# How a layer-norm and MLP kernel loads its first three raw tiles: half rows of 1,024 bytes in place of quarter pieces

## The chip, the cores and the metric

One Trainium2 chip, and on it one core: the kernel is a single program on core 0. The metric is device time in microseconds (us), from launch to end. TensorE does the matmuls, ScalarE the activation function and copies out of PSUM, VectorE (DVE) statistics, corrections and sums, GpSimd (POOL) small preparations; SyncE (SP) and ScalarE (ACT) issue the DMA transfers, each on its own queue.

## The reference

```python
B, S, D, F = 1, 2048, 1024, 3584          # all bf16
def reference(x, w1, b1, w2, b2):
    y = _layernorm(x, axis=-1)            # (x - mean) / sqrt(var + 1e-5)
    h = _gelu(jnp.einsum("bsd,df->bsf", y, w1) + b1)
    return jnp.einsum("bsf,fd->bsd", h, w2) + b2
```

## The kernel before

The 2,048 rows of `x` are 16 tiles of 128 rows, and four tiles are a block of 512 rows (`TB`). For each block the first layer makes 28 rows of `hT` (128 of the 3,584 columns of `w1` each), with eight accumulating matmuls per row, one for each 128-wide slice `dt` of D; then the second layer makes the output, and VectorE adds `b2`. Each engine's instructions stand in an order written out by hand; semaphores alone join them.

The change touches only the start, where the weights and `x` are still on their way. So that TensorE need not wait for layer-norm statistics, the first three tiles (`N_RAW`) enter the first layer as they are, transposed but not normalised. A column of ones beside them (column `RC`, 384) gives the column sums of `w1`, and VectorE corrects the results later, in PSUM, with each row's mean and deviation. Tile 3 takes the ordinary way: VectorE takes its statistics, normalises it (line 294), and only then is it transposed.

The parts of that start:

- **Loads.** `SP_FIRST_LOADS` and `ACT_FIRST_LOADS` (lines 28 and 29) are the order of issue on the two queues. `w0` to `w7` are slices dt 0 to 7 of the first seven rows of `w1`, 224 KB each. `x0p`, `x1p`, `x2p` are columns 0 to 255 of tiles 0, 1, 2 (64 KB each, 512 bytes a row); `xq` is columns 256 to 511 of all three tiles (192 KB), `xr` columns 512 to 1023 of all three (384 KB), `x3` is tile 3.
- **`warm(WARM)`, `warm(FILL)`.** 24 and 3 matmuls on constants, whose results nobody reads.
- **`pe_T`** (line 370). Transposes blocks of 128x128 on TensorE (line 378) into a PSUM bank; ScalarE copies them into `yT_sb` (line 391). A call names slices of D and tiles: `(0, 2, 1, 2)` is dt 0 and 1 of tile 1. Banks are "t", or "2_0" and "2_1", which two rows of the first wave take over afterwards.
- **`cells`** (line 518). Matmuls (line 416) of the first wave of `R` = 7 rows, for given rows, slices and tiles: 128 columns wide for one tile, 385 for all three and the ones. `first` is rows 0 to 4, `last2` rows 5 and 6, `every` all of them.
- **`act_cs`** (line 534). ScalarE copies the column sums of the wave's rows into `cs_sb` (line 536).
- **`late_row`** (line 557). Adds tile 3's part of a row, eight matmuls of 128 columns; it waits for the copies of tile 3's transposes and for `cs`. Behind late_row(0) and late_row(2) `pe_row` spreads the rows' means and deviations over the partitions (line 601), ScalarE copies them (line 604), and VectorE corrects row by row (lines 545 and 548).
- **Statistics.** VectorE takes those of the first halves (columns 0 to 511) of tiles 0, 1, 2, then of the second halves, then aggregates, then tile 3 (lines 266 and 274).

The stretch of the order that the change rewrites:

```python
        cells(first, (6,), 0, 3)
        pe_T([(0, 4, 3, 4), (4, 8, 3, 4)], "t")
        cells(first, (7,), 0, 3)
        act_cs(ps_1, 0, NB1, False)
        cells(last2, (6, 7), 0, 3)
        act_cs(ps_2, NB1, R, True)
        late_row(0)
```

## Time and profile before

| | |
|---|---|
| median of 3 runs | 397.53 us (397.34 to 397.7) |
| the profiled execution's own time | 397.77 us |
| its span, first to last instruction | 396.5 us |
| TensorE busy | 393.8 us, 1,999 matmuls |
| VectorE, ScalarE busy | 161.9 us, 84.2 us |
| DMA | 23.62 MB, nearly all of the loads in the first 57 us |

Times in the profile count from the first instruction of the span. A row of the timeline has start, duration, engine, line, operation, output and inputs, shape, count and, in brackets, the idle time of the engine ahead of it with what ended it. PE are the matmuls, PEld the weight loads that go with them; matmuls are pipelined, so that a matmul's listed duration reaches over the start of the next, and the spacing of starts is the pace. DMA issues are listed by engine with size and the time from issue to landing.

### The profile page before, as it was taken

How to read it: one execution, taken by the hardware profiler on the slowest of the kernel's cores; microseconds unless marked ns; L12 is line 12 of the kernel's file. 1: busy time of each engine (PE TensorE's matmuls, PEld its weight loads, DVE VectorE, ACT ScalarE, POOL GpSimd, SP SyncE). 2: the span in 40 equal slices, each digit the busy share in tenths (PEclk: the TensorE clock that was granted, in tenths of full speed). 3: DMA queues.
4: the chain of work that ended last, by engine and by line, in shares of the span. 5: the costliest groups of instructions: out<-in, count | busy, mean ns of one | idle time of the engine just before them, and what ended most of it. 6: DMA issues, size and time to landing. Idle time of an engine off the chain costs nothing.

```text
span 396.5 us, 4668 instructions
## 1 busy us (share of the span) xinstructions
PE 393.8 (99%) x1999; PEld 188.6 (48%) x1999; DVE 161.9 (41%) x343; ACT 84.2 (21%) x133; POOL 9.9 (2%) x28
## 2 busy tenths in 40 slices
PE   9999999999999999999999999999999999999998
PEld 7774444444444444444444444444444444444445
DVE  2798889988999705988100000001100000001011
ACT  3446430000143442000024433100003334400000
POOL 1100100002000200000000000000000000000000
DMA  7999950000000000000000000000000000000000
GB/s 243 361 378 387 385 185 15 26 26 16 26 0 2 0 0 2 26 15 26 26 15 0 0 2 0 13 15 26 14 27 13 2 0 0 2 13 26 15 26 26
DMA packets 17003, 23.62 MB, mean 60 GB/s; under 512 B 1240, under 2 KB 10584, under 8 KB 16984
## 3 DMA queue, kind: packets, MB, share of 16 engines
q1 hardware_dynamic: 16696, 23.05, 16.6%
q8 instruction: 15, 0.25, 0.3%
q10 hardware_dynamic: 288, 0.30, 0.2%
q14 instruction: 4, 0.03, 0.0%
HBM read 19.14 MB, written 4.19 MB: 59 GB/s over the span
## 4 chain that ended last, share of the span: by engine, by line
PE 99%; DVE 0%; issue 0%
PE ps L470 49%; PE ps L416 41%; PE ps_t L416 8%; PE ps L494 1%; PE ps_t L378 1%; PE ps L378 0%; PE ps_t L601 0%; DVE o_sb L481 0%
## 5 line engine op out<-in xcount | busy, mean ns | idle before, releaser
L470 PE MATMUL ps<-w_sb,hT_sb 128*128 128x512 bf16 (+2 forms) x924 | 194.1, 373 | 0.0
L416 PE MATMUL ps<-yT_sb,w_sb 128*128 128x512 bf16 (+3 forms) x862 | 167.9, 353 | 0.0
L470 PEld LDWEIGHTS ps<-w_sb,hT_sb 128*128 128x128 bf16 x924 | 89.3, 98 | 104.5
L416 PEld LDWEIGHTS ps<-yT_sb,w_sb 128*128 128x128 bf16 x862 | 80.0, 99 | 82.9
L425 ACT ACTIVATE hT_sb<-ps,b_sb 128x512 bf16<-128x512 f32 x94 | 64.3, 688 | 230.1 <-PE ps L416 217.2
L481 DVE TENSOR_TENSOR o_sb<-ps,b_sb 128x512 bf16<-128x512 f32 (+2 forms) x33 | 22.2, 674 | 198.4 <-PE ps L470 198.4
L354 DVE STREAM_TRANSPOSE yT_sb<-x_sb 32x256 bf16<-32x256 bf16 x192 | 83.7, 436 | 18.0 <-PE ps_t L416 15.0
L416 PE MATMUL ps_t<-yT_sb,w_sb 128*128 128x512 bf16 (+2 forms) x152 | 34.2, 368 | 0.0
L266 DVE BATCH_NORM_STATS2 st_sb<-x_sb 128x6 f32<-128x512 bf16 x32 | 20.8, 670 | 6.2 <-DMA x_sb<-in_x_dram 6.2
L416 PEld LDWEIGHTS ps_t<-yT_sb,w_sb 128*128 128x128 bf16 x152 | 14.6, 98 | 16.5
L425 ACT ACTIVATE hT_sb<-ps_t,b_sb 128x512 bf16<-128x512 f32 x18 | 12.4, 687 | 17.4 <-PE ps_t L416 14.6
L271 POOL TENSOR_TENSOR rstd_sb<-mv_sb,nhalf 128x1 f32<-128x1 f32 x13 | 7.1, 544 | 118.0 <-DVE mv_sb L274 117.5
L553 DVE TENSOR_TENSOR ps<-ps,row_sb 128x384 f32<-128x384 f32 x13 | 7.2, 561 | 3.1 <-PE ps L416 2.8
L294 DVE TENSOR_SCALAR x_sb<-x_sb,mv_sb,rstd_sb 128x1024 bf16<-128x1024 bf16 x13 | 7.1, 543 | 2.5 <-POOL rstd_sb L271 2.0
L545 DVE SCALAR_TENSOR_TENSOR ps<-row_sb,cs_sb,ps 128x385 f32<-128x385 f32 x11 | 6.8, 614 | 1.6 <-ACT row_sb L604 1.6
L548 DVE TENSOR_TENSOR ps<-ps,row_sb 128x385 f32<-128x385 f32 x11 | 6.2, 567 | 0.7 <-ACT row_sb L604 0.4
L391 ACT COPY yT_sb<-ps_t 128x384 bf16<-128x384 bf16 (+2 forms) x9 | 4.0, 493 | 8.2 <-PE ps_t L378 8.2
L494 PE MATMUL ps<-const-bfloat16-1.0 128*128 128x128 bf16 x27 | 3.2, 310 | 0.8 <-PEq L730 0.8
L334 DVE TENSOR_TENSOR yT_sb<-yT_sb,row_sb 128x1024 bf16<-128x1024 bf16 x3 | 3.6, 1215 | 0.0
L274 DVE BATCH_NORM_AGGREGATE mv_sb<-st_sb 128x2 f32<-128x15 f32 x16 | 3.2, 212 | 0.9
L494 PEld LDWEIGHTS ps<-const-bfloat16-1.0 128*128 128x128 bf16 x27 | 2.8, 144 | 0.8 <-issue 0.8
L378 PE MATMUL ps_t<-ident,x_sb 128*128 128x128 bf16 x28 | 2.5, 224 | 0.1
(40 smaller groups left out, 17.0 us busy)
## 6 DMA issues: line engine op xcount, KB each, us to landing
w_sb<-in_w_dram SPq DMA_DIRECT2D x4, 1792.0 KB, 18.1
out_dram<-o_sb SPq DMA_DIRECT2D x31, 128.0 KB, 1.7
x_sb<-in_x_dram SPq DMA_DIRECT2D x3, 1024.0 KB, 14.0
w_sb<-in_w_dram SPq DMA_DIRECT2D x2, 1024.0 KB, 9.5
w_sb<-in_w_dram SPq DMA_DIRECT2D x1, 2048.0 KB, 15.5
w_sb<-in_w_dram SPq DMA_DIRECT2D x7, 224.0 KB, 5.6
w_sb<-in_w_dram SPq DMA_DIRECT2D x1, 1280.0 KB, 16.3
x_sb<-in_x_dram SPq DMA_DIRECT2D x1, 384.0 KB, 5.5
```

Of the source, the lines that this page charges most:

```text
L266: return (lambda e, i=i, h=h: e.bn_stats(st_sb[:, i, 6 * h:6 * (h + 1)], x_sb[:, i, h * HC:(h + 1) * HC]), [x_ev[i][h]] + ([f"x{i}p"] if i ...
L271: pool.op(lambda e, i=i: e.tensor_tensor(out=rstd_sb[:, i:i + 1], in0=mv_sb[:, i, 1:2], in1=nhalf[:, i:i + 1], op=ALU.pow), waits=[f"mv{i} ...
L294: return (lambda e, i=i, c0=c0, c1=c1: e.tensor_scalar(out=x_sb[:, i, c0:c1], in0=x_sb[:, i, c0:c1], scalar1=mv_sb[:, i, 0:1], scalar2=rst ...
L354: res.append((lambda e, src=src, dst=dst: e.transpose(out=dst, in_=src), waits, (f"tr{i}" if lastop else None), 0.47))
L378: pe.op(lambda e, i=i, j=j, o=n * P: e.transpose(out=bap[:, o:o + P], in_=x_sb[:, i, j * P:(j + 1) * P], identity=ident[:, :]), waits=wait ...
L416: pe.op(lambda e: e.matmul(unit_bank(bank)[:, n0:n1], lhsT=w1_sb[:, dt, r * P:(r + 1) * P], rhs=yT_sb[:, buf, dt, n0:n1], start=start, sto ...
L425: act.op(lambda e, r=r, n0=n0, n1=n1, bank=bank: e.activation(out=hT_sb[:, r, n0:n1], in_=unit_bank(bank)[:, n0:n1], func=ACT.Gelu_apprx_tanh,
L470: pe.op(lambda e, st=st, ft=ft, c0=c0, c1=c1, bank=bank: e.matmul(ps_2[:, bank, 0:c1 - c0], lhsT=hT_sb[:, ft, st * P:(st + 1) * P], rhs=w2 ...
L481: crit.append((est[sig], (lambda e, ob=ob, c0=c0, c1=c1, bank=bank: e.tensor_tensor(out=o_sb[:, ob, c0:c1], in0=ps_2[:, bank, 0:c1 - c0], ...
L494: pe.op(lambda e: e.matmul(ps_1[:, 0, 0:P], lhsT=unit, rhs=unit, start=True, stop=True), waits=[gate] if gate else [])
L545: return [(lambda e: e.scalar_tensor_tensor(out=ap, in0=row_sb[:, 0, :], scalar=cs_ap[r], in1=ap, op0=ALU.mult, op1=ALU.add), [f"m1_0_{r}" ...
L553: crit.append((est[wait_ev], (lambda e: e.tensor_tensor(out=ap, in0=ap, in1=row_sb[:, 1, 0:RC], op=ALU.mult), [wait_ev, "row1"], f"sc_{r}" ...
```

## The change

Tiles 0, 1 and 2 are loaded by whole first halves, `x0a`, `x1a`, `x2a`: columns 0 to 511, 1,024 bytes a row, 128 KB each. `xq` is gone, and the order of the other loads stays. `x0a` is the first on SP, as `w0` is on ACT; `x2a` follows `w0` on ACT. All first-half statistics and the transposes of dt 0 to 3 now wait for a tile's own piece.

In TensorE's order tile 2's first transposes go into bank "t" rather than "2_1", and stand behind four of tile 0's seven cells; rows 5 and 6 follow in plain order. Tile 3's transposes move behind the first two cells of the last slice (dt 7), so that three cells of it and four of rows 5 and 6 are left between them and late_row(0), where there were five and four.

```diff
-SP_FIRST_LOADS = ("x0p", "x1p", "w1", "xq", "w2", "w3", "xr", "w4", "x3", "w5", "w6", "w7", "b1", "w8")
-ACT_FIRST_LOADS = ("w0", "x2p")
+SP_FIRST_LOADS = ("x0a", "x1a", "w1", "w2", "w3", "xr", "w4", "x3", "w5", "w6", "w7", "b1", "w8")
+ACT_FIRST_LOADS = ("w0", "x2a")
...
-            elif item[-1] == "p":
+            elif item[-1] == "a":
                 i = int(item[1:-1])
-                dma(x_sb[:, i, 0:QC], xf[i * P:(i + 1) * P, 0:QC], item, P * QC * 2)
-                x_ev[i] = ("xq", "xr")
+                dma(x_sb[:, i, 0:HC], xf[i * P:(i + 1) * P, 0:HC], item, P * HC * 2)
+                x_ev[i] = (item, "xr")
...
-                    [x_ev[i][h]] + ([f"x{i}p"] if i < N_RAW and h == 0 else []), f"st{i}_{h}", 0.65)
+                    [x_ev[i][h]], f"st{i}_{h}", 0.65)
...
-                    waits=waits + [raw_ev(i, j) if i < N_RAW else y_ev[i][j]],
+                    waits=waits + [x_ev[i][j * P // HC] if i < N_RAW else y_ev[i][j]],
...
         pe_T([(0, 2, 0, 1)], "t")
         warm(FILL)
         pe_T([(0, 2, 1, 2)], "2_0")
-        pe_T([(0, 2, 2, 3)], "2_1")
-        cells([*first, *reversed(last2)], (0,), 0, 1)
+        cells(every[:4], (0,), 0, 1)
+        pe_T([(0, 2, 2, 3)], "t")
+        cells(every[4:], (0,), 0, 1)
         cells(every, (0,), 1, 2)
         cells(every, (0,), 2, 3)
...
         cells(first, (6,), 0, 3)
+        cells(first[:2], (7,), 0, 3)
         pe_T([(0, 4, 3, 4), (4, 8, 3, 4)], "t")
-        cells(first, (7,), 0, 3)
+        cells(first[2:], (7,), 0, 3)
         act_cs(ps_1, 0, NB1, False)
         cells(last2, (6, 7), 0, 3)
```

More of the change, by code (lines that the diff above doesn't have):

```diff
@@ L111, in bass_standalone__mixer_channel_mlp__prompt_kernel @@
     assert DT == 8 and 0 < N_RAW < TPB
-    QC = 2 * P
     NR = max(R, min(RAW_ROWS, FT - 2))
@@ L212, in issue @@
         def issue(item):
-            if item in ("xq", "xr"):
-                c0, c1 = (QC, HC) if item == "xq" else (HC, D)
-                dma(x_sb[:, 0:N_RAW, c0:c1], xf[0:N_RAW * P, c0:c1].rearrange("(t p) d -> p t d", p=P), item,
-                    N_RAW * P * (c1 - c0) * 2)
-            elif item[-1] == "p":
+            if item == "xr":
+                dma(x_sb[:, 0:N_RAW, HC:D], xf[0:N_RAW * P, HC:D].rearrange("(t p) d -> p t d", p=P), item,
+                    N_RAW * P * HC * 2)
+            elif item[-1] == "a":
                 i = int(item[1:-1])
-                dma(x_sb[:, i, 0:QC], xf[i * P:(i + 1) * P, 0:QC], item, P * QC * 2)
-                x_ev[i] = ("xq", "xr")
+                dma(x_sb[:, i, 0:HC], xf[i * P:(i + 1) * P, 0:HC], item, P * HC * 2)
+                x_ev[i] = (item, "xr")
             elif item == "b1":
@@ L365, in bass_standalone__mixer_channel_mlp__prompt_kernel @@
         t_bank = {"t": ps_t[:, 0, :], "2_0": ps_2b[:, 0, :], "2_1": ps_2b[:, 1, :]}
-        def raw_ev(i, j):
-            return f"x{i}p" if j * P < QC else "xq" if j * P < HC else "xr"
         def pe_T(groups, bname):
```

## The prediction

> **What bounds the kernel now.** I read the page first: parts 1 and 4, busy time and the chain that ended last.

> ```profile
> PE 393.8 (99%) x1999; PEld 188.6 (48%) x1999; DVE 161.9 (41%) x343; ACT 84.2 (21%) x133; POOL 9.9 (2%) x28
> PE 99%; DVE 0%; issue 0%
> ```

> TensorE's own stream is the end of the kernel: the change can only save pauses between matmuls, or time that they run slowly. From the trace's list of matmul starts I subtracted the undisturbed spacing (0.163 us behind a 385-column one, 0.056 behind a 128-column one, 0.216 behind 512). From 5.9 us to the end all pauses add up to 0.40 us, and two make up 0.35 of it. The timeline of TensorE's weight loads shows both:

> ```profile
> 6.84 0.34 PEld L378 LDWEIGHTS ps_t<-ident,x_sb 128*128 128x128 bf16 x6 [0.38 <-DMA x_sb<-in_x_dram]
> 14.23 0.46 PEld L378 LDWEIGHTS ps_t<-ident,x_sb 128*128 128x128 bf16 x8 [0.39 <-issue]
> ```

> The first is the transposes of columns 256 to 511, which wait for `xq`. The matmul before started at 6.525, so the engine was free at 6.69 and began at 6.84: 0.15 us. The second is tile 3's transposes, which wait for its normalisation: free at 13.900 + 0.163 = 14.06, begun at 14.26: 0.20 us. The brackets count weight-load idle, part of which is normal.

> Next the stages of the start: us, then busy time and count of TensorE, weight loads, VectorE, ScalarE, GpSimd; granted clock; DMA share; GB/s.

> ```profile
> 2.40:3.00 0.60, 0.60 (x8) 0.60 (x7) 0.00 (x0) 0.58 (x1) 0.25 (x3) 1.00 0.98 341
> 3.60:4.00 0.40, 0.40 (x5) 0.39 (x5) 0.00 (x0) 0.03 (x1) 0.00 (x0) 1.00 0.93 314
> 4.00:4.60 0.60, 0.60 (x9) 0.59 (x7) 0.00 (x0) 0.44 (x2) 0.00 (x0) 1.00 0.40 99
> 4.60:5.20 0.60, 0.60 (x7) 0.45 (x5) 0.00 (x0) 0.55 (x2) 0.00 (x0) 1.00 0.69 109
> 5.20:5.80 0.60, 0.60 (x8) 0.60 (x7) 0.00 (x0) 0.00 (x0) 0.00 (x0) 1.00 0.79 218
> 5.80:6.40 0.60, 0.60 (x13) 0.60 (x11) 0.00 (x0) 0.00 (x0) 0.00 (x0) 1.00 1.09 352
> ```

> Two things are to be seen. TensorE gets through more 128-column matmuls per stretch behind 5.8 us than before it: their spacing falls there from 0.107 to 0.056 us, though the granted clock's column says 1.00 throughout. So a pause ahead of 5.8 costs only (0.107 - 0.056) less than it looks: each 0.107 us lost displaces one matmul, which is then done at 0.056, a factor of 0.52. And the DMA engines, at 314 to 341 GB/s before 4.0, fall to about 100 from 4.0 to 5.2, while `w1` and `xq` are on their way.

> Last, the work behind tile 3's transposes on ScalarE, and the VectorE steps ahead of them (start, duration):

> ```profile
> 14.90 1.07 ACT L391 COPY yT_sb<-ps_t 128x512 bf16<-128x512 bf16 x2 [2.07 <-PE ps_t L378]
> 15.86 0.18 ACT L536 COPY cs_sb<-ps 128x5 f32<-128x5 f32 x1
> ```

> ```profile
> 9.15 1.88 DVE L266 BATCH_NORM_STATS2 st_sb<-x_sb 128x6 f32<-128x512 bf16 x3 [0.45 <-DMA x_sb<-in_x_dram]
> ...
> 13.57 0.54 DVE L294 TENSOR_SCALAR x_sb<-x_sb,mv_sb,rstd_sb 128x1024 bf16<-128x1024 bf16 x1
> ```

> The small copy (`cs`, at line 536) ends at 16.05, and the first `late_row` starts at 16.17. That start is no wait yet: the matmul before began at 16.010, and 16.010 + 0.163 is 16.17. But the margin is only 0.12 us less the signal's own time, which an exposed wait for a ScalarE copy shows as 0.06 (copy done 5.15, matmul at 5.20). So late_row(0) can't be much over 0.06 us earlier while tile 3's transposes stay where they are.

> **The loads.** Removed are `xq` and the three 64 KB pieces; added are three of 128 KB. Bytes ahead of `w2`, `w3` and `xr` are the same (1,056 KB up to `w2`), so I leave these where they landed (7.39, 8.00, 9.12); one SP issue less (0.43 us of SP's time) brings nothing, since these issues end over 5 us ahead of the landings. `x0p` was issued at 0.79 and landed 2.64 later, at 3.43; `x1p` at 3.97, `x2p` at 4.15, `w0` at 3.72. For `x0a`, twice the bytes beside `w0`: between 3.43 (nothing lost) and 3.75 (lands with `w0`); I take 3.55, nearer the first, because the half-size piece landed 0.29 ahead of `w0`. All of `x0a`, `x1a`, `x2a` and `w0` is 608 KB against 416 before, 197 kB more; at 330 GB/s that is 0.6 us, so `x2a` lands by 4.75. For `x1a`: between 3.97 and 5.3 (caught in the thin stretch); I take 4.35, a third of the difference off `x2a`. `w1` landed at 6.25, 640 KB into the loads; now it is 832 KB in, without `xq` beside it: 5.4 to 6.5, and I take 6.2, before its matmuls need it.

> **TensorE up to 6.5 us.** The 24 warm-up matmuls end at 3.38. Before, the first transpose came at 3.56, 0.13 after the landing; now at 3.68: 0.12 us lost. Two transposes and three fillers take 5 x 0.107 = 0.53 to 4.21; tile 1's transposes wait for `x1a` until about 4.45: 0.24 lost. Four cells of tile 0 (0.43) now cover tile 2's load and its transposes; the bank of row 5 is no longer used for a transpose, so the wait for its copy (0.09 at 5.11 to 5.20) goes. Net 0.27 at the slow spacing, times 0.52: +0.14 us. Ends: no loss, -0.05 (only the bank wait goes), and +0.56 if `x1a` lands at 5.3 or later.

> **Behind 6.5 us.** Columns 256 to 511 are there already: -0.15. Tile 3's transposes stand two cells later (2 x 0.163 = 0.33): TensorE reaches them at 14.06 - 0.15 + 0.33 + 0.14 = 14.38, past 14.26, so the wait for `y` goes: -0.20. VectorE keeps its order; its first statistics start early, but its second ones still wait for `xr`, so `y` stays. But the move takes cover from the copies. From the start of tile 3's transposes to late_row(0) TensorE has 8 x 0.056 + 7 x 0.163 = 1.59 us of work (before, nine cells, 1.92), and the ScalarE chain takes 16.05 - 14.26 + 0.06 = 1.85. A new wait of 0.26 us stands ahead of late_row(0), on the `cs` copy; queued behind it are all late rows, row broadcasts and with them VectorE's corrections. Ends: 0.0, if the copies chain faster, and 0.33. Later waits have over 0.5 us of margin or move along with TensorE.

> Sum: +0.14 - 0.15 - 0.20 + 0.26 = +0.05 us. The profiled execution spans 396.5 and took 397.77, 1.27 outside the span; 0.24 over the median of 397.53. So the median should be 397.58; I say 397.6, no change. From 0.2% (0.8 us) on, a measurement of this kernel can tell a difference.

> **The rivals.** *The clock rises later (slower).* The fast spacing came at 5.8, 5.0 us after the first matmul and 2.3 after the pause that ended at 3.56. The change puts about 0.30 + 0.24 us of pauses into that stretch, where 0.18 + 0.09 were. If pauses of that size break it off, the rise comes 2.3 to 5.0 us after the one that ends at 4.45, at 6.7 to 9.4. Each us of slow spacing costs 1 - 0.52 = 0.48, so +0.4 to +1.7; I take 1.7, since the one rise that the trace shows from rest took 5.0: 399.2. It decides from a rise at 7.5 on (0.8 us). For it: nothing shows how much pause is borne. Against it: 0.27 was.
> [...]

> *The thin stretch catches the x pieces.* If the DMA engines thin out at 4.0 whatever is queued, `x1a` lands at 5.3, and `w1` after 6.5. TensorE then stands some 0.95 us more, less than half of it made up: +0.6, 398.1. For it: the fall came when the first 416 KB were through, and now 608 are wanted. Against it: then only `w1` and 512-byte rows were under way.

> *Faster.* All pauses go with nothing in their place: -0.35 - 0.14 = -0.49, 397.1. To pass 0.2% the clock must rise 0.65 us earlier as well (0.31/0.48): 396.7. Against it: the `cs` chain, and the pauses that late `x` pieces add.

> **How the numbers follow.** No change 0.59, its own range 397.1 to 398.0. Clock late 0.24, all slower. Thin stretch 0.12, a quarter of it over 0.2%. Faster 0.05. So slower 0.24 + 0.03 = 0.27, same 0.59 + 0.09 = 0.68, faster 0.05. The range must reach into the late clock to hold 8 in 10: 397.0 to 399.2.

> **What would show it.** Right: no pause ahead of the transposes of columns 256 to 511 and of tile 3; about 0.26 us ahead of late_row(0), ended by the `cs` copy; first transposes at about 3.7, tile 1's at 4.4; fast spacing from 5.8. Wrong: the spacing of 128-column matmuls still 0.107 behind 6 us; `xr` much earlier or later than 9.1; waits on `w1`.

## The result: slower by a third of a per cent, and the profile after

| | before | after |
|---|---|---|
| median of 22 runs each | 397.74 us (397.19 to 398.47) | 399.31 us (397.76 to 400.17) |
| profiled execution, its span | 397.77, 396.5 | 399.35, 398.1 |

The ratio is 1.0033, 95% interval 1.0022 to 1.0044: +1.6 us on the medians. The forecast was no change, 397.6. What came is the rival with the late clock, put at 399.2. The median of 22 lies 0.1 us past the upper end of the range, 399.2; the ratio times the 397.53 of the start is 398.8, inside it. The range reaches that far only to take in the rival: the forecast's own, 397.1 to 398.0, is missed. The single times after fall into two groups: seven at 397.76 to 397.90, one at 398.5, and fourteen at 399.09 to 400.17. Before, all lie within 1.3 us.

Page of the kernel after, parts 1 and 4:

```profile
PE 394.6 (99%) x1999; PEld 189.3 (48%) x1999; DVE 162.0 (41%) x343; ACT 84.3 (21%) x133; POOL 9.8 (2%) x28
PE 98%; DMA 1%; DVE 0%; issue 0%; ACT 0%
```

TensorE is still the end of the kernel, but a DMA now stands in its chain with 1%. The timeline shows where: the transposes of tile 0 and of tile 1, each behind a load.

```profile
4.21 0.37 PE L373 MATMUL ps_t<-ident,x_sb 128*128 128x128 bf16 x2 [0.67 <-DMA x_sb<-in_x_dram]
...
4.87 0.39 PE L373 MATMUL ps<-ident,x_sb 128*128 128x128 bf16 x2
```

The last warm-up matmul starts at 3.23 as before, and its place of 0.107 ends at 3.34. So TensorE stood 0.87 us ahead of the first transposes (before 0.22). The prediction has 3.38 for that end, and so 0.18 for the pause before; the difference of 0.65 is the same. Ahead of the second transposes it stood 0.17 us: the third filler started at 4.59, its place ended at 4.70. The stages of the start:

```profile
3.60:4.20 0.60, 0.00 (x0) 0.02 (x1) 0.10 (x1) 0.00 (x0) 0.00 (x0) 1.00 1.08 387
...
5.20:5.80 0.60, 0.60 (x9) 0.60 (x8) 0.60 (x2) 0.37 (x1) 0.00 (x0) 1.00 0.98 350
5.80:6.40 0.60, 0.60 (x8) 0.60 (x7) 0.33 (x1) 0.37 (x1) 0.00 (x0) 1.00 1.00 319
7.00:7.60 0.60, 0.60 (x8) 0.60 (x7) 0.00 (x0) 0.00 (x0) 0.00 (x0) 1.00 1.09 399
```

From 5.8 to 6.4 eight matmuls are under way where there were 13. The spacing is 0.107 us until 8.37 and 0.056 from there; before, that fell at 5.85. The granted clock's column says 1.00 throughout again. From 3.6 to 4.2 no matmul runs at all. The DMA engines keep 319 to 399 GB/s in these rows; the thin stretch of before (109 GB/s from 4.6 to 5.2) has shrunk to 224 to 260 there.

Behind that, the waits that were to go are gone, and the new one is there. Weight loads of TensorE, then ScalarE:

```profile
17.65 0.39 PEld L411 LDWEIGHTS ps<-yT_sb,w_sb 128*128 128x128 bf16 x7 [0.48 <-ACT cs_sb L531]
```

```profile
16.46 1.07 ACT L386 COPY yT_sb<-ps_t 128x512 bf16<-128x512 bf16 x2 [2.20 <-PE ps_t L373]
17.41 0.40 ACT L531 COPY cs_sb<-ps 128x5 f32<-128x5 f32 x2
```

The first copy of column sums ends at 17.60, and late_row(0) starts at 17.65; the matmul before it ended its place at 17.40, so the wait is 0.25 us.

### The profile page after: what moved, and what is told of

It reads as the page before. It is cut to its first block, busy times and chain, and to the rows that moved or that the text cites. A ratio compares the mean times of both kernels' runs of the same rounds, so it can differ in the third digit from the quotient of the medians.

```text
span 398.1 us, 4666 instructions
## 1 busy us (share of the span) xinstructions
PE 394.6 (99%) x1999; PEld 189.3 (48%) x1999; DVE 162.0 (41%) x343; ACT 84.3 (21%) x133; POOL 9.8 (2%) x28
## 4 chain that ended last, share of the span: by engine, by line
PE 98%; DMA 1%; DVE 0%; issue 0%; ACT 0%
PE ps L465 49%; PE ps L411 41%; PE ps_t L411 8%; DMA x_sb<-in_x_dram 1%; PE ps_t L373 1%; PE ps L373 0%; PE ps_t L596 0%; PE ps L489 0%; DVE o_sb L476 0%; ACT cs_sb L531 0%
```

## Experiments

Times are medians against the kernel before, run on the same chip (397.76 to 397.90). "Rise" is where the spacing of matmuls halves in the profiled execution, or where TensorE starts again if it stood then.

**The pause filled.** `-WARM = 24` `+WARM = 32` in the kernel after.

> The kernel after with 32 warm-up matmuls on constants ahead of the first transposes, where it has 24: 8 x 0.107 = 0.85 us more, so that they end at 4.23, when the first x piece is there (4.07 and the signal), and TensorE's first real work starts as late as in the kernel after. Theory (the pauses ahead of the x pieces delay the rise of TensorE's clock): the pause of 0.8 us is filled, the fast spacing comes at 5.8 to 6.5 instead of 8.4 and mostly in every execution, and the time falls by 0.9 to 1.2 us to about 398.1 to 398.4 or lower. Rival (the later loads themselves, with the waits that follow from them, cost the time): nothing of that moves, 399.3.

398.28 us (397.78 to 399.08), ratio 1.0010 (1.0002 to 1.0019); rise at 5.2. The first transposes start at 4.37, later even than in the kernel after, and the loads are the same (`x0a` at 4.24). About 1.0 of the 1.6 us is gone with eight matmuls that compute nothing, and so is the late group: apart from the profiled execution at 399.08 (span 396.8), no time is over 398.55. So the late loads as such don't carry the loss. What stays, 0.5 us, I put down to useful work that starts later. That isn't shown: with 28 warm-ups, below, it starts as late, at 4.40, and only 0.1 us stays.

**A pause alone.** `-WARM = 24` `+WARM = 16` in the kernel before, whose loads stay.

> The kernel before with 16 warm-up matmuls instead of 24: they end at 2.53, and TensorE stands 1.03 us until the first x piece, as the loads stay as they are. Theory (pauses delay the clock): the fast spacing comes up to 2.6 us later in most executions, the times spread into two groups, and the median rises by 0.8 to 1.7 us, to 398.5 to 399.4. Rival (the later loads cost the time, not the pause): no load moves and no useful matmul moves, 397.7 within 0.2.

398.46 us (397.91 to 398.98), ratio 1.0018 (1.0009 to 1.0026); rise at 8.1. Timeline of TensorE:

```profile
0.82 1.86 PE L494 MATMUL ps<-const-bfloat16-1.0 128*128 128x128 bf16 x16 [0.82 <-PEq L730]
3.51 0.37 PE L378 MATMUL ps_t<-ident,x_sb 128*128 128x128 bf16 x2 [0.83 <-DMA x_sb<-in_x_dram]
```

The first transposes come at 3.51, as in the kernel before, every useful matmul has its data when it had it or before, and the kernel is still slower by 0.7 us. The pause, 1.04 us here, delays the clock. The sum closes here too: the clock rises 2.2 us later, at 0.48 each 1.06 us, and with TensorE that late the waits for columns 256 to 511 and for tile 3 (0.15 + 0.20) are gone, though the loads are the old ones: 0.71, and the span grew from 396.54 to 397.22, by 0.68. The median came out just under the expected 398.5, and the two groups aren't to be seen.

**Tile 3's transposes alone.** In the kernel before:

```diff
         cells(first, (6,), 0, 3)
+        cells(first[:2], (7,), 0, 3)
         pe_T([(0, 4, 3, 4), (4, 8, 3, 4)], "t")
-        cells(first, (7,), 0, 3)
+        cells(first[2:], (7,), 0, 3)
```

> The kernel before with only tile 3's transposes moved two cells later. Theory (the clock carries the loss): the wait for tile 3's normalisation (0.20 us) goes and one for the small copy of column sums comes in its place; late_row(0) at 14.39 + 1.85 = 16.24 instead of 16.17, so +0.07 us, 397.7 to 397.9. Rival (the move of the transposes is what costs): a good part of the 1.6 us, at 398.5 or more.

397.93 us, ratio 1.0004 (0.9995 to 1.0013): within what was expected, and not to be told from before. The wait for the normalisation is gone and the one on `cs` has come, 0.25 us, ended by `cs` at line 536.

**The same edit undone in the kernel after.**

> The kernel after with tile 3's transposes back behind the cells of slice 6. Theory (the clock carries the loss): the wait of 0.25 us ahead of late_row(0) goes, the normalised tile 3 is there long before, so -0.2 us, and the late clock stays: about 399.1, still in two groups. Rival (the move of the transposes is what costs): back near 397.8.

398.79 us (397.55 to 400.01), ratio 1.0023 (1.0008 to 1.0038), six times at 397.55 to 398.12 and six at 399.47 to 400.01. The early group starts 0.2 us lower than in the kernel after, as expected, and the trace has no wait on `cs`; of the late group that can't be said. The groups stay, and the median between them says little. In the profiled execution the clock rises at 10.0, and TensorE doesn't wait for the normalisation of tile 3 either.

**A smaller pause.** `-WARM = 24` `+WARM = 20` in the kernel before, and `-WARM = 24` `+WARM = 28` in the kernel after.

> The kernel before with 20 warm-up matmuls: TensorE stands 0.6 us ahead of the first x piece, between the 0.2 of the kernel before and the 1.04 of the one with 16. Window theory (the clock is released at the end of a stretch of about 3.4 us in which TensorE stood no more than some limit, and those stretches run freely of the kernel; the traces put the limit between 0.40 us, which was borne, and 1.04, which was not): if 0.6 + 0.1 is borne, the times are those of before, 397.8 within 0.2; if not, the median is at 398.3 or more as with 16. Rival (any pause delays the rise by about its own length or more): half of the loss of 16 warm-ups, 398.1.

No trace up to then shows the stretch of about 3.4 us that the first expectation takes; that of the split load, below, has 3.41.

398.02 us (397.49 to 398.82), ratio 1.0007 (0.9998 to 1.0015): between the two expectations, and not to be told from the kernel before. The rise is at 7.2 in the trace (398.30 us).

> The kernel after with 28 warm-up matmuls: 0.43 us of the first pause is filled, 0.45 to 0.5 stays, and 0.17 ahead of tile 1. Window theory (up to about 0.8 us in one window is borne): no late group, at most 398.8, median about 398.2, like 32 warm-ups. Rival (the delay grows with the pause): halfway between 398.28 with 32 and 399.31 with 24, 398.8, with times over 399.

397.98 us (397.68 to 398.45), ratio 1.0004 (0.9995 to 1.0012), rise at 5.8. The late group is gone with half the pause filled, and the time is that of 32 warm-ups or less. A loss in proportion to the pause (398.8) is out.

**The kernel after, twice more.**

> The kernel after once more, for one more trace of it. Window theory: the loads land as they did (x0a at 4.1, x1a at 4.8) and the pauses are the same, but the fast spacing comes at another time: either by 4.9 (time about 397.8) or at 8.3 to 10.2 (399.1 to 400.2). Rival (a set number of undisturbed matmuls): 8.4 again, 399.3.

> The kernel after a third time, for the same question: the fast spacing by 4.9 with about 397.8, or at 8.3 to 10.2 with 399.1 to 400.2 (windows that run freely of the kernel); 8.4 and 399.3 again (a set number of matmuls).

399.17 with the rise at 8.0, and 399.48 with 8.6. `x0a` landed at 4.12 and 4.20, and the pauses are near those of the first trace (together 1.08 and 1.16 us, there 1.04); the rises differ by 0.6 us, and the times with them. So no set number of matmuls releases the clock, which would have given 8.4 again. The first is earlier than the 8.3 that I had given. No early execution was caught.

**Tile 0 in two pieces.** In the kernel after, `x0p` being columns 0 to 255 of tile 0 and `x0q` columns 256 to 511 (shown is the start of the order of loads; the first transposes wait for `x0p` alone):

```diff
-SP_FIRST_LOADS = ("x0a", "x1a", "w1", ...
+SP_FIRST_LOADS = ("x0p", "x0q", "x1a", "w1", ...
```

> The kernel after with tile 0's first half in two pieces of 512-byte rows, one behind the other on SP (64 KB each), the first of which alone the first transposes wait for. Theory (the first load is late because it is twice as long beside w0): the first piece lands at 3.4 to 3.5 as before, the first transposes start at 3.6, and the pause moves to tile 1's, which land at 4.8 or later: from 4.1 on, 0.7 us or more. By the window theory 0.2 + 0.7 is about as much as 1.04, so the loss stays largely, 398.5 to 399.3, in two groups. Rival (the pause ahead of the first transposes alone matters): 397.7 to 397.9. Where the second piece lands tells what the row length costs: at 4.07 the bytes count alone, later the shorter rows cost.

400.28 us (398.05 to 401.68, six runs), ratio 1.0060 (1.0038 to 1.0083): worse than any expectation. The first piece landed at 3.48 and the second at 4.0, but `x1a`, behind them, at 5.8: the thin stretch is back (74 to 110 GB/s from 4.2 to 4.8). TensorE stood 2.0 us ahead of tile 1's transposes. This trace holds a record of the granted clock, and so do five others, from the clock's first change on. Ahead of that, and in the traces without a record, the column reads 1.00 even where the spacing is slow, 0.107 us. The pause, and the column by stages:

```profile
5.87 0.28 PE L377 MATMUL ps<-ident,x_sb 128*128 128x128 bf16 x2 [1.79 <-DMA x_sb<-in_x_dram]
```

```profile
6.66:7.02 0.36, 0.36 (x8) 0.36 (x9) 0.36 (x1) 0.23 (x1) 0.00 (x0) 1.00 1.06 351
7.15:7.80 0.65, 0.65 (x9) 0.65 (x7) 0.00 (x0) 0.00 (x0) 0.00 (x0) 0.50 1.05 357
9.00:10.30 1.30, 1.30 (x7) 0.69 (x6) 1.30 (x3) 0.86 (x2) 0.00 (x0) 0.50 1.05 397
10.60:11.60 1.00, 1.00 (x8) 0.60 (x7) 1.00 (x6) 0.00 (x0) 0.42 (x1) 1.00 1.10 368
```

The clock rises at 3.675, in the middle of the transposes, falls to one half at 7.088 in the middle of a steady run of matmuls, and rises again at 10.502. Both distances are 3.41 us. No load lands and no wait of TensorE ends at these times, so I read the clock as set at fixed steps, 3.41 us here, by what TensorE did in the step that ends. The other records bear the steps out: each runs from the rise to the fall behind the kernel's end, 392.533 us in four traces and 389.119 in the one with tile 3's transposes put back (and here, from 10.502), which is 115 and 114 steps of 3.4133 us, wherever the rise fell.

Here a step that ended at 3.675 released the clock with 0.82 us ahead of the first matmul (0.56 of it inside the step) and a pause of 0.28 in it, 0.84 together; in the second trace of the kernel after, the step from 1.1 to 4.6 held a pause of 0.92 us and didn't. All 14 traces fit a limit between the two, if the steps are counted back from each rise: in eight the clock rose at the end of a step with 0.31 to 0.84 us of idle time, and in the other six the step ahead of the one that released it held 0.92 to 1.16. Idle time ahead of the first matmul counts in them: with 20 warm-ups the step that ended at 3.8 held 0.64 us of pause and 0.43 ahead of the first matmul, and the clock rose a step later, at 7.2.

**What delays `x0a`.** Two orders of the loads in the kernel after: all on SP (`x0a`, `w0`, `x1a`, `x2a`, `w1`, ...), and `w0` behind `x2a` on ScalarE's queue.

> The kernel after with all its first loads on SP's queue, one behind the other: x0a, w0, x1a, x2a, w1 and so on; ScalarE issues none. Theory (w0 beside it on the other queue is what puts x0a 0.5 us behind the estimate of 3.55): x0a lands at 3.3 to 3.6, the first pause falls to 0.2 to 0.4, w0 and x1a come at 4.0 to 4.5. The pauses of a window then add up to 0.4 to 0.8, which is borne, and the time is 397.7 to 398.2 in one group. Rival (the bytes of the first transfer in the slow first half microsecond, whoever else is there): x0a at 3.9 or later, 399 in two groups.

> The kernel after with w0 behind x2a on ScalarE's queue, so that x0a shares the DMA engines with rows of 1,024 bytes at first. Theory (w0's longer rows beside it delay x0a): x0a lands at 3.5 to 3.8, x2a likewise at 4.0, w0 at 4.6 to 4.9; the first pause falls to 0.3 to 0.5, and another one of 0.3 to 0.6 comes ahead of the first cells, which need w0. Both together are near the limit: 398.0 to 399.3, partly in two groups. Rival (any company on the other queue delays it as much): x0a at 4.07 still, 399.3 or more.

The issue of `x0a`, KB and us to landing, of the kernel after, with all on SP, and with `w0` behind `x2a`:

```profile
x_sb<-in_x_dram SPq DMA_DIRECT2D x1, 128.0 KB, 3.3
```

```profile
x_sb<-in_x_dram SPq DMA_DIRECT2D x1, 128.0 KB, 2.2
```

```profile
x_sb<-in_x_dram SPq DMA_DIRECT2D x1, 128.0 KB, 2.7
```

So the company on the other queue sets most of it: landed at 3.02 alone, 3.47 beside `x2a` (128 KB in rows of 1,024 bytes), 4.07 beside `w0` (224 KB in rows of 1,792). Beside `w0` five more traces have 4.12 to 4.26; beside `x2a` the one below has 3.18. Whether the other load's bytes or its row length count these runs don't separate. Neither order helps, since the pause moves: with all on SP `x2a` lands at 5.6 and TensorE stands 0.8 us for it (399.18 us, ratio 1.0034, 1.0021 to 1.0048, five times up to 398.51, one at 399.18 and five from 399.84); with `w0` last it stands three times, 0.97 us together (399.14, ratio 1.0028, 1.0012 to 1.0044, six times up to 398.44 and six from 399.84). Both traces are of the early groups: 398.29 with the rise at 4.7, and with `w0` last 397.58 with the rise at 3.8, during the fillers.

**Put together.** `w0` behind `x2a`, tile 3's transposes where they were before, 26 warm-ups, and at the start of TensorE's order:

```diff
         pe_T([(0, 2, 0, 1)], "t")
+        pe_T([(0, 2, 2, 3)], "2_0")
         warm(FILL)
-        pe_T([(0, 2, 1, 2)], "2_0")
-        cells(every[:4], (0,), 0, 1)
-        pe_T([(0, 2, 2, 3)], "t")
-        cells(every[4:], (0,), 0, 1)
+        pe_T([(0, 2, 1, 2)], "2_1")
+        warm(2)
+        cells([*first, *reversed(last2)], (0,), 0, 1)
```

> A version put together from what the runs showed: the loads with w0 behind x2a, tile 3's transposes where they were before, 26 warm-up matmuls, tile 2's first transposes ahead of tile 1's (its piece lands at 3.6), and the pauses ahead of x1a and of w0 filled with 3 and 2 matmuls on constants. Theory: x0a at 3.5, x1a at 4.2, w0 at 4.7, the first cells at 4.8 instead of 4.47 (+0.16 us), no wait for columns 256 to 511 (-0.15), none for tile 3's normalisation, since xr lands over 1 us earlier (-0.20), the bank wait gone (-0.05), and no new wait ahead of late_row(0): -0.2 us, about 397.6, in one group, at most just to be told from before. Rival (w1 and the later weights are caught by a thin stretch of the loads, as with all loads on one queue): 398 or more.

397.86 us against 397.90, ratio 0.9995 (0.9986 to 1.0004): the whole loss is undone, in one group (397.24 to 397.91), but the kernel before isn't beaten. `x1a` landed at 5.1 in the profiled execution, not 4.2, so the loads aren't steady from run to run. TensorE stood 1.16 us for it:

```profile
3.83 0.34 PE L489 MATMUL ps<-const-bfloat16-1.0 128*128 128x128 bf16 x3
5.17 0.29 PE L373 MATMUL ps<-ident,x_sb 128*128 128x128 bf16 x2 [1.00 <-DMA x_sb<-in_x_dram]
```

The clock had risen at 3.7 by the spacing, and it stayed up, though the step to 7.1 held 1.30 us of pauses: 128-column matmuls behind 7.15 are 0.056 apart. So the released clock bore 1.30 us in this trace, where one that was still slow, in the second trace of the kernel after, hadn't borne 0.92.

## Where the prediction failed, and where it held

The term that failed is the first pause: `x0a` was taken at 3.55, "nearer the first" bound, and landed at 4.07, past the upper bound of 3.75. That bound is the old landing of `w0`, 3.72: I let `x0a` grow to twice the bytes and left `w0` where it was. `x0a` did land ahead of `w0`, by 0.23 us (0.29 before), but `w0` itself came at 4.30; the trace after has 242 GB/s from 2.4 to 3.0 where that of before has 341. `x1a` (4.35) landed at 4.82 and `x2a` (by 4.75) at 5.02. So the pauses ahead of tiles 0 and 1 came to 0.87 + 0.17 us, not 0.30 + 0.24. Two of the prediction's own signs of being wrong came: the spacing was 0.107 behind 6 us, and `xr` was early.

That decided between the cases: 1.04 us in one step of 3.41 us is over what a clock that was still slow bore in the traces (0.84, and 0.92 not), and 0.54 would not have been. The filled pauses, the pause alone and the step of the split load show this; the limit between 0.84 and 0.92 is as narrow as that by one trace on each side. The steps run freely (three traces of this kernel have the rise at 8.37, 8.0 and 8.6), so where they lie in an execution is chance. In the kernel after, a step that ends ahead of or inside the pauses could still release the clock, and then the time would be 397.8: the early group. Otherwise it takes the next one, from 8.0 to 10.0 in the traces of this kernel and of the one with tile 3's transposes put back. That only the late group makes the loss is shown by the times; that its members all rise late is seen in the three traces of the kernel after.

The sizes of the other terms held. The wait for columns 256 to 511 went (-0.15), that for tile 3 too (-0.20), and 0.25 came ahead of late_row(0), forecast at 0.26. But the traces don't show that the change took the two waits away: TensorE came to them over a us later than before, and in the pause alone, with the old loads and the old order, they are gone as well. And with `xr` early, tile 3's transposes need not have moved: put back, they have no wait, and the early group, where TensorE isn't late, starts 0.2 us lower. So in this kernel the move brought only the 0.25. The factor of 0.52 for pauses at the slow spacing and the price of 0.48 per us of late clock close the sum for the two profiled executions: pauses (0.87 - 0.22 + 0.17 - 0.09) x 0.52 = 0.38, waits -0.15 - 0.20 + 0.25 = -0.10, clock (8.37 - 5.85) x 0.48 = 1.21; together 1.49, measured 396.54 to 398.08, 1.54.

The rival had the mechanism and took its price from the wrong end of its rows: 1.7 with a rise at 9.4, where the first trace has 8.4. That its 399.2 lies so near the median is luck in part: 1.21 for the clock and 0.38 for the pauses, forecast at 0.14, together come near the 1.7. Of the other rivals, the thin stretch didn't catch the x pieces. It went with the rows of 512 bytes (245 GB/s from 4.6 to 5.2, and 361 and 369 in the two repeats, where before has 109) and came back with them in the split load. That those rows cause it isn't settled: with all loads on one queue, without a row of 512 bytes, the rate fell to 139 from 4.2 to 4.8, and `x2a` and `w1` were late as well. `xr` landed at 8.32 and not at 9.12. (The reason given for leaving it, issues that end over 5 us ahead of the landings, holds for `xr` alone: for `w2` and `w3` it was 4.3 and 4.4. And the upper end given for the pauses at the start, +0.56, comes to 0.63 by the prediction's own numbers, (0.27 + 0.95) x 0.52; the sum doesn't use it.) VectorE's normalisation of tile 3 ended 0.8 us earlier for it, and nobody waited for that:

```profile
8.34 1.88 DVE L264 BATCH_NORM_STATS2 st_sb<-x_sb 128x6 f32<-128x512 bf16 x3 [2.21 <-DMA x_sb<-in_x_dram]
...
12.77 0.54 DVE L292 TENSOR_SCALAR x_sb<-x_sb,mv_sb,rstd_sb 128x1024 bf16<-128x1024 bf16 x1
```

## What to carry to other kernels

While TensorE's clock was still slow, pauses cost more than their length here: 0.73 us more of them made 1.59 us, 1.21 of it by the clock. By the traces what counted was how much idle time fell into one step of 3.41 us, and four more matmuls on constants in the pause were worth more (28 in place of 24: ratio 1.0004 in place of 1.0033, about 1.2 us) than the waits that the larger loads were to save later (0.15 + 0.20). Ask of a load at the start not only how many bytes it has but what shares the DMA engines with it: the 128 KB of `x0a` landed at 3.02 alone and at 4.07 beside `w0`. And look at the single times: the two groups, 397.76 to 397.90 and 399.09 to 400.17, were the sign that something decides which runs freely of the kernel.
